# Hoisted LayerNorm statistics, a split transpose eviction and TensorE warm-up matmuls at the start of a one-core transformer block

## The chip, the cores and the metric

The kernel runs on one core of a Trainium2 chip. The metric is device time in microseconds of the whole program; lower is better. The 31 executions of the kernel before that stand beside the experiments lie within 0.36 % of each other (865.16 to 868.29 us), those of each other kernel within 0.27 %, so differences of 1 us (0.1 %) need several rounds and, better, the trace. All runs compared below are of the fast state (none is over 1.5 % above the fastest of its kernel; the largest excess is 0.37 %).

Engines are named as in the profile: PE (TensorE matmul), PEld (its weight load), ACT (ScalarE), DVE (VectorE), POOL (GpSimd), SP (SyncE, which issues the DMAs here).

## The reference

A pre-LayerNorm linear-attention block (32 heads of 32) and a gated ReLU block, bf16, 2048 tokens of width 1024, hidden width 3584:

```python
x = A_x
h  = x + _A_ref(_layernorm(x), A_wqkv, A_wo)      # pk, pq = phi(k), phi(q); kv = pk^T v; o = pq kv / (pq z)
h2 = h + _B_ref(_layernorm(h), B_W_gate, B_W_up, B_W_down)   # (relu(x Wg) * (x Wu)) Wd
# phi(t) = where(t > 0, t + 1, exp(t)) + 1e-6
```

Only the first 25 us matter: LayerNorm of the first row tiles of x (128 rows each), their transposes, and the first k projections.

## The kernel before

The program is a list of operations for each engine, and semaphores carry the dependencies between engines. On DVE the order of emission is the order of execution in the traces: in the kernel before, tile 3's x had landed at 10.5 us (issued at 3.25, 7.2 us to landing), yet its statistics, which need nothing else, ran at 18.63, behind tile 2's normalize at 17.24, before which DVE stood idle for 1.36 us.

```python
NX1 = 4                                    # buffers for x tiles

def layernorm(src_full, src_chunk_bufs, dst_ap, dst_buf, norm_eng, name):
    # DVE: bn_stats x2, bn_aggr;  POOL: ve = var + eps, rstd = ve ** -0.5, nmr = -mean * rstd
    ... (cut)
    PL.add("dve", lambda e: e.tensor_scalar(out=dst_ap, in0=src_full, scalar1=rstd[:, k, :],
                                            scalar2=nmr[:, k, :], op0=ALU.mult, op1=ALU.add), ...)

def ln1(st):
    i = st % NX1
    layernorm(x1[:, i, :], B_x1[i], xn[:, st % 2, :], B_xn[st % 2], "dve", "ln1_%d" % st)
    if st + NX1 < NST:
        load_x1(st + NX1)                  # tile 4 goes into tile 0's buffer

def T1(st):                                # 8 transposes on PE, one eviction on ACT
    (b,) = alloc_banks(P1_POOL)
    transpose8(xn[:, st % 2, :], [B_xn[st % 2]], b, NDC, "T1_%d" % st)
    evac_T("act", b, NDC, xnT[:, :, st * P:(st + 1) * P], [B_xnT[st]], "evT1_%d" % st)

def kvp_piece(st, nt):                     # 8 matmuls of 128x512, then phi: ACT exp, two DVE operations
    ... (cut)

load_x1(0, split=True); load_x1(1); load_wkv(0)     # all on the one SP queue (cut to its order)
load_x1(2); load_x1(3); load_wkv(1); load_wkv(2); load_wkv(3)

for st in range(min(2, WB)):               # WB = 4
    ln1(st)
for st in range(WB):
    T1(st)
    kvp_piece(st, 0)
    if st + 2 < WB:
        ln1(st + 2)
if WB < NST:
    ln1(WB)                                # tile 4
for nt in range(1, NKV):                   # the other pieces of tiles 0 to 3: PE has plenty to do from here
    for st in range(WB):
        kvp_piece(st, nt)
        ... (cut)
```

Of the kernel before, what the change touches and what calls it, by code (L numbers as in the profile page):

```python
# [5 lines left out]
dt = mybir.dt  # L6
ALU = mybir.AluOpType
ACTF = mybir.ActivationFunctionType
# [118 lines left out]
def bass_sequential_preLN__linear_attn_block__glu_gated_reglu__prompt_kernel(  # L127
# [10 lines left out]
    _, S, D = A_x.shape  # L138
# [3 lines left out]
    P = 128  # L142
# [3 lines left out]
    NW = min(512, D)  # L146
# [32 lines left out]
    with es:  # L179
        def sb(name, shape, dtype):  # L180
            return es.enter_context(nc.sbuf_tensor(name, list(shape), dtype))
# [43 lines left out]
        oT = RE[:, o0:o0 + NG * SBW].rearrange("p (a b) -> p a b", a=NG)  # L225
        hnT = [hnT0, hnT1]

        hsb = sb("hsb", [P, 2, STB, D], bf16)
        xn = sb("xn", [P, 2, D], bf16)
        Et = sb("Et", [P, 3, EW], bf16)  # L230
        E2t = sb("E2t", [P, 3, EW], bf16)
# [7 lines left out]
        ones_col = sb("ones_col", [P, 1], bf16)  # L239
        neghalf = sb("neghalf", [P, 1], f32)  # L240
        warm = sb("warm", [P, 8], f32)
        ip_i = sb("ip_i", [P, P], dt.int32)
        jp_i = sb("jp_i", [P, P], dt.int32)
        st6 = sb("st6", [P, NSTAT, NBC * 6], f32)
        mv = sb("mv", [P, NSTAT, 2], f32)
        ve = sb("ve", [P, NSTAT, 1], f32)
# [10 lines left out]
        def bank(b, w=512):  # L257
            return ps[:, b, 0:w]

        def bank_bf(b):  # L260
            return ps[:, b, :].bitcast(bf16).rearrange("p (a b) -> p a b", b=P)
# [17 lines left out]
        def bufs(name, n):  # L279
            return [_Buf("%s%d" % (name, i)) for i in range(n)]  # L280
# [1 line left out]
        B_bank = bufs("bank", 8)  # L282
        B_x1 = [bufs("x1_%d_" % i, NBC) for i in range(NX1)]
        B_xn = bufs("xn_", 2)
        B_xnT = bufs("xnT_", NST)
        B_wkv = bufs("wkv_", NKV)
        B_wq = bufs("wq_", ND2)
        B_wo = bufs("wo_", ND2)
# [28 lines left out]
        B_ones = _Buf("ones")  # L317
        B_neghalf = _Buf("neghalf")
        B_warm = _Buf("warm")
        B_ipi = _Buf("ipi")  # L320
        B_jpi = _Buf("jpi")

# [5 lines left out]
        def alloc_banks(pool, n=1):  # L328
            cand = sorted(pool, key=lambda b: bank_last[b])
            got = cand[:n]  # L330
            assert len(got) == n
            for b in got:
                bank_clock[0] += 1
                bank_last[b] = bank_clock[0]
            return got

        def touch_bank(b):
            bank_clock[0] += 1
            bank_last[b] = bank_clock[0]

        PL.add("pool", lambda e: e.memset(ident[:], 1.0), writes=[B_ident], name="ident1")
        PL.add(
            "pool",
# [100 lines left out]
        def mm(out_ap, lhsT, rhs, start, stop, reads, bbuf, name, skip=False):  # L444
            return PL.add(
                "pe",
                lambda e: e.matmul(out_ap, lhsT, rhs, start=start, stop=stop, skip_group_check=skip),  # L447
                reads=reads, writes=[bbuf], name=name,
            )
# [12 lines left out]
        def evac_T(eng, b, nblk, dst_ap, dst_bufs, name):  # L462
            src = bank_bf(b)[:, 0:nblk, :]
            if eng == "act":
                PL.add("act", lambda e: e.activation(out=dst_ap, in_=src, func=ACTF.Identity),  # L465
                       reads=[B_bank[b]], writes=dst_bufs, name=name)
            else:
                PL.add("dve", lambda e: e.tensor_copy(out=dst_ap, in_=src),
                       reads=[B_bank[b]], writes=dst_bufs, name=name)

        stat_ctr = [0]

        def layernorm(src_full, src_chunk_bufs, dst_ap, dst_buf, norm_eng, name):
            k = stat_ctr[0] % NSTAT
            stat_ctr[0] += 1
            for c in range(NBC):
                PL.add("dve", lambda e, c=c: e.bn_stats(out=st6[:, k, c * 6:(c + 1) * 6],  # L477
                                                        in_=src_full[:, c * BCH:(c + 1) * BCH]),
                       reads=[src_chunk_bufs[c]], writes=[B_st6[k][c]], name=name + "_bn")
            PL.add("dve", lambda e: e.bn_aggr(out=mv[:, k, :], in_=st6[:, k, :]),  # L480
                   reads=B_st6[k], writes=[B_mv[k]], name=name + "_aggr")
            PL.add("pool", lambda e: e.tensor_scalar(out=ve[:, k, :], in0=mv[:, k, 1:2], scalar1=EPS,  # L482
                                                     scalar2=None, op0=ALU.add),
                   reads=[B_mv[k]], writes=[B_ve[k]], name=name + "_ve")
            PL.add("pool", lambda e: e.tensor_tensor(out=rstd[:, k, :], in0=ve[:, k, :], in1=neghalf[:],  # L485
                                                     op=ALU.pow),
                   reads=[B_ve[k], B_neghalf], writes=[B_rstd[k]], name=name + "_rstd")
            PL.add("pool", lambda e: e.tensor_scalar(out=nmr[:, k, :], in0=mv[:, k, 0:1],  # L488
                                                     scalar1=rstd[:, k, :], scalar2=-1.0,
                                                     op0=ALU.mult, op1=ALU.mult),  # L490
                   reads=[B_mv[k], B_rstd[k]], writes=[B_nmr[k]], name=name + "_nmr")
            if norm_eng == "act":
                PL.add("act", lambda e: e.activation(out=dst_ap, in_=src_full, func=ACTF.Identity,
                                                     scale=rstd[:, k, :], bias=nmr[:, k, :]),
                       reads=list(src_chunk_bufs) + [B_rstd[k], B_nmr[k]], writes=[dst_buf], name=name + "_norm")
            else:
                PL.add("dve", lambda e: e.tensor_scalar(out=dst_ap, in0=src_full, scalar1=rstd[:, k, :],  # L497
                                                        scalar2=nmr[:, k, :], op0=ALU.mult, op1=ALU.add),
                       reads=list(src_chunk_bufs) + [B_rstd[k], B_nmr[k]], writes=[dst_buf], name=name + "_norm")

        phi_ctr = [0]

# [20 lines left out]
            col = g * P  # L523
            return ps[:, KVB[col // 512], (col % 512):(col % 512) + P]

        def ln1(st):
            i = st % NX1
            layernorm(x1[:, i, :], B_x1[i], xn[:, st % 2, :], B_xn[st % 2], "dve", "ln1_%d" % st)
            if st + NX1 < NST:
                load_x1(st + NX1)  # L530

        def T1(st):
            (b,) = alloc_banks(P1_POOL)
            transpose8(xn[:, st % 2, :], [B_xn[st % 2]], b, NDC, "T1_%d" % st)
            evac_T("act", b, NDC, xnT[:, :, st * P:(st + 1) * P], [B_xnT[st]], "evT1_%d" % st)

        def kvp_piece(st, nt):
            slot = st % NPK
            (b,) = alloc_banks(P1_POOL)
            for dc in range(NDC):  # L540
                mm(bank(b, NW), xnT[:, dc, st * P:(st + 1) * P], wkv[:, dc, nt * NW:(nt + 1) * NW],
                   dc == 0, dc == NDC - 1, [B_xnT[st], B_wkv[nt]], B_bank[b], "kvp_%d_%d" % (st, nt))
            if nt < ND2:
                phi(b, NW, pk[:, slot, nt * NW:(nt + 1) * NW], B_pk[slot][nt], "k_%d_%d" % (st, nt))
            else:
                j = nt - ND2
                PL.add("act", lambda e, b=b, j=j: e.activation(out=vv[:, slot, j * NW:(j + 1) * NW],  # L547
                                                               in_=bank(b, NW), func=ACTF.Identity),
                       reads=[B_bank[b]], writes=[B_v[slot][j]], name="v_%d_%d" % (st, j))
# [38 lines left out]
        def a1(sb_, ct, pool):  # L588
            (b,) = alloc_banks(pool)
            for dc in range(NDC):  # L590
                mm(bank(b, SBW), wq[:, dc, ct * P:(ct + 1) * P], xnT[:, dc, sb_ * SBW:(sb_ + 1) * SBW],
                   dc == 0, dc == NDC - 1, [B_wq[(ct * P) // NW]] + B_xnT[sb_ * STB:(sb_ + 1) * STB],
                   B_bank[b], "a1_%d_%d" % (sb_, ct))
            phi(b, SBW, pqT[:, sb_, ct, :], B_pqT[sb_][ct], "q_%d_%d" % (sb_, ct))

# [161 lines left out]
                if bulk:  # L757
                    bulk.pop(0)()

        for st in range(min(2, WB)):  # L760
            ln1(st)
        for st in range(WB):
            T1(st)
            kvp_piece(st, 0)
            if st + 2 < WB:
                ln1(st + 2)
        if WB < NST:
            ln1(WB)
        for nt in range(1, NKV):
            for st in range(WB):  # L770
                kvp_piece(st, nt)
                if nt == NKV - 1 and st >= 1:
                    kvacc(st - 1)
            if nt == 1:
                if WB < NST:
                    T1(WB)
                if WB + 1 < NST:
                    ln1(WB + 1)
        if NKV == 1:
            for st in range(1, WB):  # L780
                kvacc(st - 1)
            if WB < NST:
                T1(WB)
            if WB + 1 < NST:
                ln1(WB + 1)
        for st in range(WB, NST):
            if st + 1 < NST:
                T1(st + 1)
            if st + 2 < NST:
                ln1(st + 2)  # L790
            trickle(2)
            kvp(st)
            kvacc(st - 1)
# [126 lines left out]
```

## Time and profile before

| | before |
|---|---|
| device time, median of 4 (lowest to highest) | 865.92 us (865.58 to 866.59) |
| profiled span | 863.8 us |
| PE busy | 847.2 us, 98 % |
| PE busy between 25 and 855 us | 829.68 of 830 us |

The table of stretches gives, for each stretch of the span, its length, then the busy us (and instructions) of PE, PEld, DVE, ACT and POOL, the granted PE clock (the share of full clock speed that the trace records; 1.00 is full), the DMA share and GB/s. Of the kernel before:

```profile
20.00:25.00 5.00, 3.25 (x21) 1.51 (x20) 1.68 (x4) 1.62 (x2) 1.05 (x3) 1.00 0.24 73
25.00:30.00 5.00, 5.00 (x25) 2.29 (x24) 2.39 (x5) 1.79 (x3) 0.81 (x3) 1.00 0.01 3
25.00:855.00 830.00, 829.68 (x4522) 397.82 (x4521) 259.75 (x487) 166.53 (x249) 29.49 (x84) 1.00 0.39 124
```

PE is full from 25 us on, so nothing that happens later on another engine can shorten the time. What can be won lies before. The timeline of PE shows it, each line with start, length, instructions, and in brackets the idle time before them with what ended it (L457 are transposes, L447 projections). Of the kernel before:

```profile
6.70 1.01 PE L457 MATMUL ps<-ident,xn 128*128 128x128 bf16 x8 [6.70 <-DVE xn L497]
9.16 3.59 PE L447 MATMUL ps<-RB,RA 128*128 128x512 bf16 x8 [1.45 <-DMA RB<-in_A_wqkv_dram]
12.55 1.06 PE L457 MATMUL ps<-ident,xn 128*128 128x128 bf16 x8
14.72 1.90 PE L447 MATMUL ps<-RB,RA 128*128 128x512 bf16 x8 [1.12 <-ACT RA L465]
17.84 0.62 PE L457 MATMUL ps<-ident,xn 128*128 128x128 bf16 x8 [1.22 <-DVE xn L497]
19.58 1.90 PE L447 MATMUL ps<-RB,RA 128*128 128x512 bf16 x8 [1.11 <-ACT RA L465]
22.11 0.62 PE L457 MATMUL ps<-ident,xn 128*128 128x128 bf16 x8 [0.63 <-DVE xn L497]
23.85 8.81 PE L447 MATMUL ps<-RB,RA 128*128 128x512 bf16 x40 [1.12 <-ACT RA L465]
```

There are four pairs of transposes and projection, one for each tile. Eight projection matmuls take 3.59 us the first time, starting 427 ns apart, and 1.90 us later, 216 ns apart: PE starts at half clock. (The clock column reads 1.00 there all the same: the trace holds no clock record before 14.27 us. The spacing of the matmuls is the evidence: in the changed kernel it is 427 ns where the record reads 0.50, from 22.91 to 26.32 us, and 216 ns where it reads 1.00.) **The number to watch is 23.85 us**, the start of tile 3's projection: from there PE waits for 0.3 us in all until the end.

In the chain of waits (start, length, what), the last of those four steps reads as follows before the change (the pieces named "issue", under 0.1 us each, are left out here and below):

```profile
21.21 0.28 POOL nmr L488
21.51 0.56 DVE xn L497
22.11 0.64 PE ps L457 x8
22.77 1.03 ACT RA L465
23.85 8.81 PE ps L447 x40
```

Statistics, three POOL steps, normalize, transposes and eviction stand one after the other. Last, the load of tile 4, of which the kernel before takes no notice: the first line is from the timeline of SP (issue and its length), the second from the DMA view (count, size, us from issue to landing):

```profile
10.45 3.27 SPq L375 DMA_DIRECT2D RE<-in_A_x_dram  x1
RE<-in_A_x_dram SPq DMA_DIRECT2D x1, 256.0 KB, 9.7
```

It is issued at 10.45 us, behind three weight loads of 1 MB each, and lands at 20.1.

### The profile page before, as it was taken

To read this page: it belongs to the slowest core of one execution; us is meant where nothing else is said; L and a number is where in the kernel's file an instruction comes from. 1 tells how busy PE (TensorE), PEld (TensorE's weight loads), DVE (VectorE), ACT (ScalarE), POOL (GpSimd) and SP (SyncE) were. 2 spreads that over 40 slices of the span, in tenths; PEclk is the share of its full clock that TensorE was granted. 3 is DMA by queue.
4 is the path that set the end of the run, shared out by engine and by line. 5 is a ranking of instruction groups with operands and counts; after the bars stand their busy time and mean duration, and the time that the engine had idled before them with its cause. 6 is when DMAs were issued, how large, how long until landed. Compare 5 with 4: busy or idle time off the path is not lost.

```text
span 863.8 us, 10965 instructions
## 1 busy us (share of the span) xinstructions
PE 847.2 (98%) x4608; PEld 405.9 (47%) x4608; DVE 274.3 (32%) x517; ACT 173.9 (20%) x258; POOL 34.9 (4%) x107
## 2 busy tenths in 40 slices
PE   4999999999999999999999999999999999999998
PEld 2455555554544444445444444454444444444443
DVE  4534444766534321115432201343411012112111
ACT  2334443332322211001222100022221001111100
POOL 2101100000000000000000000000000000000000
PEclk9999999999999999999999999999999999999999
DMA  8156500000144336553333555334354654363052
GB/s 279 46 190 201 187 1 1 1 13 25 30 148 160 113 105 213 172 166 126 122 110 116 188 180 185 123 99 133 99 183 129 211 171 152 116 195 99 26 173 94
DMA packets 105536, 109.75 MB, mean 127 GB/s; under 512 B 2960, under 2 KB 101520, under 8 KB 105488
## 3 DMA queue, kind: packets, MB, share of 16 engines
q1 hardware_dynamic: 105488, 109.06, 39.7%
q8 instruction: 36, 0.59, 0.3%
q14 instruction: 12, 0.10, 0.0%
HBM read 104.86 MB, written 4.19 MB: 126 GB/s over the span
## 4 chain that ended last, share of the span: by engine, by line
PE 97%; DVE 1%; DMA 1%; POOL 0%; issue 0%; ACT 0%; SPq 0%; DVEq 0%
PE ps L447 95%; PE ps L457 2%; DMA RB<-in_A_wqkv_dram 1%; DVE st L477 0%; POOL rstd L485 0%; DVE RE L512 0%; SPq L375 0%; DVE xn L497 0%; ACT RA L465 0%; POOL nmr L488 0%; POOL ve L482 0%; DVE RC L705 0%; DVE hsb L648 0%; DVE mv L480 0%; ACT Et L507 0%
## 5 line engine op out<-in xcount | busy, mean ns | idle before, releaser
L447 PE MATMUL ps<-RE,gring 128*128 128x512 bf16 x896 | 198.9, 379 | 0.0
L447 PE MATMUL ps<-RC,gring 128*128 128x512 bf16 x896 | 196.3, 379 | 0.0
L447 PE MATMUL ps<-wdring,RA 128*128 128x512 bf16 x896 | 194.0, 379 | 0.0
L680 DVE TENSOR_TENSOR RA<-RC,ps 128x512 bf16<-128x512 bf16 x112 | 77.0, 687 | 262.1 <-PE ps L447 262.1
L678 ACT ACTIVATE RC<-ps 128x512 bf16<-128x512 f32 x112 | 66.9, 597 | 461.9 <-PE ps L447 461.9
L447 PEld LDWEIGHTS ps<-wdring,RA 128*128 128x128 bf16 x896 | 87.7, 98 | 105.7
L447 PEld LDWEIGHTS ps<-RC,gring 128*128 128x128 bf16 x896 | 87.0, 98 | 103.0
L447 PEld LDWEIGHTS ps<-RE,gring 128*128 128x128 bf16 x896 | 86.3, 98 | 100.1
L447 PE MATMUL ps<-RB,RA 128*128 128x512 bf16 x512 | 115.3, 383 | 4.8 <-ACT RA L465 3.3
L447 PEld LDWEIGHTS ps<-RB,RA 128*128 128x128 bf16 x512 | 49.4, 98 | 62.6 <-ACT RA L465 4.0
L705 DVE TENSOR_TENSOR RC<-ps,hsb 128x512 bf16<-128x512 f32 x32 | 20.1, 684 | 176.9 <-PE ps L447 176.9
L447 PE MATMUL ps<-RA,RC 128*128 128x512 bf16 x256 | 58.0, 379 | 0.0
L447 PE MATMUL ps<-wo,RE 128*128 128x512 bf16 x256 | 57.9, 379 | 0.0
L507 ACT ACTIVATE Et<-ps 128x512 bf16<-128x512 f32 x64 | 38.2, 597 | 88.5 <-PE ps L447 55.6
L509 DVE TENSOR_SCALAR E2t<-Et 128x512 bf16<-128x512 bf16 x64 | 18.6, 291 | 66.8 <-ACT Et L507 66.7
L447 PEld LDWEIGHTS ps<-wo,RE 128*128 128x128 bf16 x256 | 25.0, 98 | 30.2
L447 PEld LDWEIGHTS ps<-RA,RC 128*128 128x128 bf16 x256 | 24.3, 98 | 27.2
L648 DVE TENSOR_TENSOR hsb<-ps,x 128x512 bf16<-128x512 f32 x32 | 22.1, 691 | 28.8 <-PE ps L447 28.6
L482 POOL TENSOR_SCALAR ve<-mv 128x1 f32<-128x1 f32 x32 | 7.1, 221 | 580.3 <-DVE mv L480 580.3
L465 ACT ACTIVATE RE<-ps 128x1024 bf16<-128x1024 bf16 x24 | 24.5, 1022 | 24.7 <-PE ps L457 24.7
L457 PE MATMUL ps<-ident,xn 128*128 128x128 bf16 x256 | 20.4, 225 | 8.9 <-DVE xn L497 8.9
L547 ACT ACTIVATE RE<-ps 128x512 bf16<-128x512 f32 x32 | 19.1, 597 | 36.3 <-PE ps L447 36.3
(45 smaller groups left out, 323.1 us busy)
## 6 DMA issues: line engine op xcount, KB each, us to landing
gring<-in_B_W_gate_dram SPq DMA_DIRECT2D x28, 1024.0 KB, 5.4
gring<-in_B_W_up_dram SPq DMA_DIRECT2D x28, 1024.0 KB, 7.5
wdring<-in_B_W_down_dram SPq DMA_DIRECT2D x56, 512.0 KB, 3.6
RB<-in_A_wqkv_dram SPq DMA_DIRECT2D x4, 1024.0 KB, 10.9
x<-in_A_x_dram SPq DMA_DIRECT2D x16, 256.0 KB, 2.6
out_dram<-RC SPq DMA_DIRECT2D x32, 128.0 KB, 3.6
RE<-in_A_x_dram SPq DMA_DIRECT2D x15, 256.0 KB, 3.0
RC<-in_A_wqkv_dram SPq DMA_DIRECT2D x2, 1024.0 KB, 6.6
```

What stands on the lines that cost most here:

```text
L447: lambda e: e.matmul(out_ap, lhsT, rhs, start=start, stop=stop, skip_group_check=skip),
L457: lambda e, i=i: e.transpose(tb[:, i, :], src_ap[:, i * P:(i + 1) * P], ident[:]),
L465: PL.add("act", lambda e: e.activation(out=dst_ap, in_=src, func=ACTF.Identity), reads=[B_bank[b]], writes=dst_bufs, name=name)
L482: PL.add("pool", lambda e: e.tensor_scalar(out=ve[:, k, :], in0=mv[:, k, 1:2], scalar1=EPS, scalar2=None, op0=ALU.add), reads=[B_mv[k]], w ...
L507: PL.add("act", lambda e: e.activation(out=Et[:, k, 0:w], in_=src, func=ACTF.Exp), reads=[B_bank[b]], writes=[B_E[k]], name=name + "_exp")
L509: PL.add("dve", lambda e: e.tensor_scalar(out=E2t[:, k, 0:w], in0=Et[:, k, 0:w], scalar1=1.0, scalar2=1e-6, op0=ALU.min, op1=ALU.add), rea ...
L547: PL.add("act", lambda e, b=b, j=j: e.activation(out=vv[:, slot, j * NW:(j + 1) * NW], in_=bank(b, NW), func=ACTF.Identity), reads=[B_bank ...
L648: PL.add("dve", lambda e, b=b, nt=nt: e.tensor_tensor(out=hsb[:, hs, j, nt * NW:(nt + 1) * NW], in0=bank(b, NW), in1=x2[:, xs, nt * NW:(nt ...
L678: PL.add("act", lambda e: e.activation(out=rg[:, k, :], in_=bank(ga, SBW), func=ACTF.Relu), reads=[B_bank[ga]], writes=[B_rg[k]], name="rg ...
L680: PL.add("dve", lambda e: e.tensor_tensor(out=hhT[:, ft, :], in0=rg[:, k, :], in1=bank(gb, SBW), op=ALU.mult), reads=[B_rg[k], B_bank[gb]] ...
L705: PL.add("dve", lambda e, j=j, k=k: e.tensor_tensor(out=outst[:, k, :], in0=bank(banks4[j], NW), in1=hsb[:, hs, j, dh * NW:(dh + 1) * NW], ...
```

## The change

Its intent is to fill the start of the program: (1) dummy matmuls on a zero tile, so that PE is at full clock when the real work comes; (2) statistics of a tile emitted one tile ahead of its normalize, so that DVE need not wait for POOL; (3) the eviction of the transposes in two halves, so that the projection's first four matmuls may start after the first half.

```diff
+        RF = sb("RF", [P, max(2 * STB * D, 1024)], bf16)   # the h buffer; the zero tile shares it
+        zeros_t = RF[:, 0:512]
...
+        PL.add("pool", lambda e: e.memset(zeros_t[:], 0.0), writes=[B_zeros], name="zeros")
...
-        def ln1(st):
+        def ln1_stats(st):
             i = st % NX1
-            layernorm(x1[:, i, :], B_x1[i], xn[:, st % 2, :], B_xn[st % 2], "dve", "ln1_%d" % st)
+            ln1_norms[st] = layernorm(x1[:, i, :], B_x1[i], xn[:, st % 2, :], B_xn[st % 2], "dve",
+                                      "ln1_%d" % st, defer=True)
+
+        def ln1_norm(st):
+            ln1_norms.pop(st)()
             if st + NX1 < NST:
                 load_x1(st + NX1)
...
+            if split and NDC >= 2:
+                src_ = bank_bf(b)
+                PL.add("act", lambda e: e.activation(out=xnT[:, 0:HDC, st * P:(st + 1) * P], in_=src_[:, 0:HDC, :],
+                                                     func=ACTF.Identity), ...)     # first half
+                PL.add("act", ...)                                                 # second half
...
+        def pe_dummies(n):
+            (b,) = alloc_banks(P1_POOL)
+            for _ in range(n):
+                mm(bank(b, 512), zeros_t[:, 0:P], zeros_t[:, 0:512], True, True, [B_zeros], B_bank[b], "dummy")
...
-        for st in range(min(2, WB)):
-            ln1(st)
+        NDUM0, NDUM1 = 14, 5
+        pe_dummies(NDUM0)
+        ln1_stats(0)
+        if WB > 1:
+            ln1_stats(1)
+        ln1_norm(0)
         for st in range(WB):
-            T1(st)
+            T1(st, split=True)
+            if st == 0:
+                pe_dummies(NDUM1)
+            if st + 2 < NST:
+                ln1_stats(st + 2)
+            if st + 1 < NST:
+                ln1_norm(st + 1)
             kvp_piece(st, 0)
-            if st + 2 < WB:
-                ln1(st + 2)
-        if WB < NST:
-            ln1(WB)
... (later tiles: statistics one tile earlier in the same way)
```

## The prediction

> **What bounds the kernel now.** TensorE. The page has PE busy 847.2 of 863.8 us; the stretch table gives 829.68 busy of 830 us between 25 and 855 us. Only the first 25 us have idle PE time that this change touches: 11.65 us busy there. The timeline shows why: T1 of tile 0 at 6.70 waits for its normalize, the first projection at 9.16 for wkv_0's landing, then each of tiles 1 to 3 pays phi, statistics, three POOL steps, normalize, transposes and eviction in series. The last PE gap ends at 23.85, when tile 3's first projection starts. After that PE is never short of work, so the change is worth what it moves 23.85, and no more.
>
> **What it removes and adds, costed from the trace.**
> - Clock: the first eight projection matmuls take 3.61 us, later eights 1.90; the transposes 1.01 to 1.06, later 0.62. [...] Fourteen dummies (about 4.5 to 6 us, estimated) should remove the slow eights: about 2.1 us in all.
> - Hoisted statistics: normalize no longer waits 1.36 us for POOL in tiles 2 and 3.
> - Split eviction: 1.02 us becomes about 0.6 before the first four matmuls may start, 0.4 a tile.
> Together some 5 us, if the inputs were there. They aren't.
>
> **What it moves into the way.** VectorE runs in order, and the hoisted statistics now stand before an earlier tile's normalize, waiting for a DMA. From issue times plus times to landing in the DMA view: tile 1 lands at 6.1, tile 2 at 9.8, tile 3 at 10.5, and tile 4, issued at 10.45 behind three 1 MB weight loads on the same queue, at 20.1.
> - stats(1) before norm(0): norm 0 ends near 8.25 instead of 6.55. T1 of tile 0 then follows, then five dummies, so the first projection starts near 10.0 instead of 9.16, but runs in 1.75 us instead of 3.6.
> - stats(2) before norm(1): norm 1 ends near 11.9 instead of 9.9; T1 of tile 1 starts at 12.0 (before 12.55).
> - Tile 2's projection starts near 16.8 (before 19.58): the gain shows here, almost 3 us.
> - stats(4) before norm(3): it cannot start before 20.1. Then 1.28 + 0.21 + 0.05 us statistics, 0.55 normalize: norm 3 ends at 22.2, T1 of tile 3 starts at 22.3 (before 22.11) and tile 3's projection at 23.6 (before 23.85).
> So the whole gain is given back waiting for tile 4's load; 0.25 us remain, from the split eviction less the late normalize.
>
> **Prediction.** 865.8 us, range 864.8 to 867.6. Faster by over 2%: 0.005; within 2%: 0.99; slower: 0.005.
>
> **What would show it.** In the timeline: BN statistics starting at about 6.1, 9.8 and 20.1, each released by a DMA; PE idle from about 18.5 to 22.3; the first projection's eight matmuls in about 1.8 us; the 25 to 855 stretch as full as before; the load of tile 4 in the chain of waits in place of POOL steps.
>
> **What would make it wrong.** [...] if the clock falls back, tile 3's transposes and projections run at half speed and the time is 1 to 2.5 us worse (about one chance in four; no trace yet shows a fallback). If tile 4 lands earlier, by changed order on the queue, up to 3 us could be gained. The aliasing of the zero tile with the h buffer and the moved banks should cost nothing, as both are idle then.

## The result, and the profile after

| | before | after |
|---|---|---|
| device time, median (lowest to highest) | 866.17 us, 13 runs (865.34 to 868.34) | 866.93 us, 9 runs (866.02 to 867.67) |
| profiled span | 863.8 us | 865.2 us |
| PE busy | 847.2 us | 852.4 us |
| tile 3's projection starts | 23.85 us | 24.13 us |
| granted clock of the whole span | 1.000 | 0.998 |

The ratio after/before is 1.0006, with a 95 % interval from 0.9997 to 1.0015. (Ratios are the mean time of one kernel's fast runs over that of the other's fast runs of the same rounds, so not quite the ratio of the medians.) Nothing was gained; the interval also holds a small loss. The 5.2 us more of busy PE are, on balance, dummies. One warning on these rows: the profiled execution of before held full clock (1.000), and most of its other executions did not (0.998 in 20 of 31, see e4). That is the likely reason why the spans differ by 1.4 us and the medians by only 0.8.

The stretches of the changed kernel, same columns:

```profile
20.00:25.00 5.00, 1.68 (x11) 0.87 (x12) 4.26 (x10) 1.08 (x2) 1.39 (x3) 0.79 0.19 60
25.00:30.00 5.00, 5.00 (x22) 2.17 (x21) 1.76 (x5) 1.19 (x2) 1.23 (x3) 0.87 0.23 56
25.00:855.00 830.00, 829.68 (x4519) 397.81 (x4518) 255.68 (x481) 166.53 (x249) 30.43 (x81) 1.00 0.39 124
```

From 25 us on PE is as full as before, but the granted clock in the first two stretches is 0.79 and 0.87. "Busy" does not tell fast from slow. (The profile's own 40 slices are 21.6 us long, and their clock row prints 9 throughout: the fall is too short to be seen there.) The timeline of PE of the changed kernel, without the lines between that bear on nothing here (dummies and projections are L451, transposes L461):

```profile
1.36 5.39 PE L451 MATMUL ps<-RF 128*128 128x512 bf16 x14 [1.36 <-POOL RF L344]
7.44 0.61 PE L461 MATMUL ps<-ident,xn 128*128 128x128 bf16 x8 [0.68 <-POOL ve L486]
9.66 1.90 PE L451 MATMUL ps<-RB,RA 128*128 128x512 bf16 x8 [0.53 <-DMA RB<-in_A_wqkv_dram]
13.61 1.90 PE L451 MATMUL ps<-RB,RA 128*128 128x512 bf16 x8 [0.69 <-ACT RA L562]
16.69 1.90 PE L451 MATMUL ps<-RB,RA 128*128 128x512 bf16 x8 [0.73 <-ACT RA L562]
22.63 0.81 PE L461 MATMUL ps<-ident,xn 128*128 128x128 bf16 x8 [4.05 <-DVE xn L504]
24.13 9.87 PE L451 MATMUL ps<-RB,RA 128*128 128x512 bf16 x40 [0.69 <-ACT RA L562]
```

The parts do what they were meant to do: the first projection takes 1.90 us instead of 3.59, the eviction wait is 0.69 to 0.73 instead of 1.12, and tile 2's projection starts at 16.69 instead of 19.58. The change is 2.9 us ahead there. Then PE is idle for 4.05 us, and behind the gap the transposes take 0.81 instead of 0.62 us and the 40 projection matmuls 9.87 instead of 8.81. Five lines of the timeline, four of DVE and one of POOL (15.92), show what PE waited for:

```profile
5.35 1.29 DVE L481 BATCH_NORM_STATS2 st<-RE 128x6 f32<-128x512 bf16 x2 [0.65 <-DMA RE<-in_A_x_dram]
10.30 1.29 DVE L481 BATCH_NORM_STATS2 st<-RE 128x6 f32<-128x512 bf16 x2 [3.01 <-DMA RE<-in_A_x_dram]
15.92 0.26 POOL L492 TENSOR_SCALAR nmr<-mv,rstd 128x1 f32<-128x1 f32 x1
20.64 1.28 DVE L481 BATCH_NORM_STATS2 st<-RE 128x6 f32<-128x512 bf16 x2 [3.44 <-DMA RE<-in_A_x_dram]
22.08 0.49 DVE L504 TENSOR_SCALAR xn<-RE,rstd,nmr 128x1024 bf16<-128x1024 bf16 x1
```

Tile 3's scale and shift were ready at 16.18 us (15.92 + 0.26), but its normalize runs at 22.08: in DVE's list it stands behind the statistics of tile 4, and these wait for tile 4's load. In the chain of waits the load has taken the place of the POOL steps (a 0.04 us piece of DVE at 21.95 is left out too):

```profile
10.88 9.73 DMA RE<-in_A_x_dram
20.64 1.30 DVE st L481 x2
22.08 0.51 DVE xn L504
22.63 0.83 PE ps L461 x8
24.13 9.87 PE ps L451 x40
```

The sum closes: tile 3's projection starts 0.28 us later (24.13 against 23.85) and the 40 matmuls take 1.06 us longer; together 1.34 us, and the profiled spans differ by 1.4 us.

### The profile page after: what moved, and what is told of

It reads as the page before. It is cut to its first block, busy times and chain, and to the rows that moved or that the text cites. A ratio compares the mean times of both kernels' runs of the same rounds, so it can differ in the third digit from the quotient of the medians.

```text
span 865.2 us, 11008 instructions
## 1 busy us (share of the span) xinstructions
PE 852.4 (99%) x4627; PEld 407.5 (47%) x4627; DVE 272.7 (32%) x517; ACT 174.0 (20%) x262; POOL 38.3 (4%) x108
## 4 chain that ended last, share of the span: by engine, by line
PE 96%; DMA 1%; SPq 1%; DVE 1%; issue 0%; POOL 0%; ACT 0%; DVEq 0%
PE ps L451 94%; PE ps L461 2%; DMA RE<-in_A_x_dram 1%; SPq L379 1%; DVE st L481 0%; DVE xn L504 0%; DVE RC L750 0%; DVE RF L693 0%; ACT RA L562 0%; POOL rstd L489 0%; POOL nmr L492 0%; DVE mv L484 0%; POOL ve L486 0%; DVEq L112 0%; SPq L112 0%
## 5 line engine op out<-in xcount | busy, mean ns | idle before, releaser
L451 PE MATMUL ps<-RE,gring 128*128 128x512 bf16 x896 | 198.9, 379 | 0.0
L451 PE MATMUL ps<-RC,gring 128*128 128x512 bf16 x896 | 196.3, 379 | 0.0
L451 PE MATMUL ps<-wdring,RA 128*128 128x512 bf16 x896 | 194.0, 379 | 0.0
L451 PEld LDWEIGHTS ps<-wdring,RA 128*128 128x128 bf16 x896 | 87.6, 98 | 105.8
L451 PEld LDWEIGHTS ps<-RC,gring 128*128 128x128 bf16 x896 | 87.0, 98 | 102.9
L451 PEld LDWEIGHTS ps<-RE,gring 128*128 128x128 bf16 x896 | 86.3, 98 | 100.1
L451 PE MATMUL ps<-RB,RA 128*128 128x512 bf16 x512 | 114.7, 382 | 2.6 <-ACT RA L562 2.1
L451 PEld LDWEIGHTS ps<-RB,RA 128*128 128x128 bf16 x512 | 49.3, 98 | 60.5 <-ACT RA L562 2.7
L750 DVE TENSOR_TENSOR RC<-ps,RF 128x512 bf16<-128x512 f32 x32 | 20.2, 684 | 176.9 <-PE ps L451 176.9
L451 PE MATMUL ps<-RA,RC 128*128 128x512 bf16 x256 | 58.0, 379 | 0.0
L451 PE MATMUL ps<-wo,RE 128*128 128x512 bf16 x256 | 57.9, 379 | 0.0
L451 PEld LDWEIGHTS ps<-wo,RE 128*128 128x128 bf16 x256 | 25.0, 98 | 30.2
L451 PEld LDWEIGHTS ps<-RA,RC 128*128 128x128 bf16 x256 | 24.3, 98 | 27.1
L486 POOL TENSOR_SCALAR ve<-mv 128x1 f32<-128x1 f32 x32 | 10.0, 311 | 578.3 <-DVE mv L484 578.3
L693 DVE TENSOR_TENSOR RF<-ps,x 128x512 bf16<-128x512 f32 x32 | 22.1, 691 | 28.8 <-PE ps L451 28.6
L461 PE MATMUL ps<-ident,xn 128*128 128x128 bf16 x256 | 19.7, 220 | 5.8 <-DVE xn L504 5.1
```

What stands on the lines that cost most here:

```text
L451: lambda e: e.matmul(out_ap, lhsT, rhs, start=start, stop=stop, skip_group_check=skip),
L461: lambda e, i=i: e.transpose(tb[:, i, :], src_ap[:, i * P:(i + 1) * P], ident[:]),
L486: PL.add("pool", lambda e: e.tensor_scalar(out=ve[:, k, :], in0=mv[:, k, 1:2], scalar1=EPS, scalar2=None, op0=ALU.add), reads=[B_mv[k]], w ...
L693: PL.add("dve", lambda e, b=b, nt=nt: e.tensor_tensor(out=hsb[:, hs, j, nt * NW:(nt + 1) * NW], in0=bank(b, NW), in1=x2[:, xs, nt * NW:(nt ...
L750: PL.add("dve", lambda e, j=j, k=k: e.tensor_tensor(out=outst[:, k, :], in0=bank(banks4[j], NW), in1=hsb[:, hs, j, dh * NW:(dh + 1) * NW], ...
```

## The experiments

Two theories. **Theory A**: the gain is given back because tile 4's hoisted statistics wait for a load and hold up tile 3's normalize. **Theory C**: on top of that, the idle gap makes PE's clock fall back, which costs over 1 us. Rivals: the load only happens to land when other work is done (B); the dummies delay the first projection (D); the split evictions harm or help by themselves (E, F).

The results together; ratios are to the kernel before in the same rounds.

| kernel | median us | ratio (95 % interval) |
|---|---|---|
| the change (first measurement) | 866.93 | 1.0006 (0.9997 to 1.0015) |
| the change again (e9) | 867.05 | 1.0008 (0.9996 to 1.0020) |
| change, tile 4's statistics late (e1) | 860.74 | 0.9938 (0.9925 to 0.9950) |
| change, fifth x buffer (e2) | 860.90 | 0.9941 (0.9929 to 0.9954) |
| change, gap filled with dummies (e3) | 864.83 | 0.9985 (0.9971 to 1.0000) |
| change without dummies (e4) | 865.67 | 0.9992 (0.9978 to 1.0007) |
| before + dummies (e5) | 863.99 | 0.9977 (0.9963 to 0.9991) |
| before + split eviction (e6) | 864.82 | 0.9985 (0.9972 to 0.9999) |
| e1 without dummies (e7) | 863.01 | 0.9964 (0.9950 to 0.9978) |
| pipelined by arrival (e8) | 858.31 | 0.9911 (0.9896 to 0.9926) |
| hoisting alone (e10) | 865.67 | 0.9997 (0.9985 to 1.0009) |
| e8 without dummies (e11) | 860.75 | 0.9941 (0.9929 to 0.9953) |

All gave correct results, and all are within 2 % of before. Each experiment was run in 5 rounds.

### e1: the same change, tile 4's statistics behind tile 3's normalize

```diff
         for st in range(WB):
             T1(st, split=True)
             ...
-            if st + 2 < NST:
+            late = st + 2 >= NX1
+            if st + 2 < NST and not late:
                 ln1_stats(st + 2)
-            if st + 1 < NST:
+            if late:
+                for s_ in ([3] if st == 2 else [4, 5]):
+                    if s_ == 3:
+                        ln1_norm(3)
+                    else:
+                        ln1_stats(s_)
+                if st == 3:
+                    ln1_norm(4)
+            elif st + 1 < NST:
                 ln1_norm(st + 1)
             kvp_piece(st, 0)
```

> The changed kernel with one order altered on VectorE: statistics of tile 4 come after the normalize of tile 3 (which had been ready since about 16 us), everything else kept. Theory A (the gain is given back waiting for tile 4's load at 20.6 us): transposes of tile 3 start at about 18.6 us instead of 22.63, tile 3's first projection at about 19.9 instead of 24.13, no clock fallback (granted clock 1.00 at 20 to 30 us), time 4.0 us under before, that is about 862.2. Rival B (the early stage is limited by PE, phi and eviction work, and the load only happens to land then): the projection moves by under 1 us and the time stays within 1 us of the changed kernel.

Measured: 860.74 us, ratio 0.9938: 5.1 us under before by the medians (865.88 there), where 4.0 were expected. The timeline of PE of e1, tile 3's transposes and projection:

```profile
17.95 0.61 PE L461 MATMUL ps<-ident,xn 128*128 128x128 bf16 x8
19.29 8.81 PE L451 MATMUL ps<-RB,RA 128*128 128x512 bf16 x39 [0.73 <-ACT RA L562]
```

No idle time stands before the transposes, and the clock is 1.00 throughout. Moving three DVE instructions was worth 6 us against the change. Rival B falls.

### e2: the same order, but the load moved

A fifth buffer lets tile 4 be loaded ahead of the later weight loads. It lies in the h buffer, which is idle at that time.

```diff
-        NX1 = 4
+        NX1 = 5
+        NX1R = 4                       # four in the old place
...
+        def x1(i):
+            return x1r[:, i, :] if i < NX1R else RF[:, 1024:1024 + D]
```

> The changed kernel with its order kept and the load moved: a fifth x buffer (in the h buffer's idle space) lets tile 4 be loaded ahead of the three later weight loads, so that it lands near 11.2 us instead of 20.6. Theory A: statistics of tile 4 start at about 17.2 us without a wait, transposes of tile 3 at about 19.4, its projection at about 20.6, no fallback, 3.2 us under before, about 863. A is only right if this and the altered order both gain; if the altered order gains and this does not, it is the place of the statistics' own 1.5 us on VectorE that counts and not the load. Rival B: within 1 us of the changed kernel.

Measured: 860.90 us, ratio 0.9941. Tile 4's statistics, in the order that had cost everything, no longer wait, as the timelines of SP (first line: the load is issued at 3.73 us instead of 10.88) and of DVE show (no idle time in brackets):

```profile
3.73 0.46 SPq L384 DMA_DIRECT2D RF<-in_A_x_dram  x1
15.71 1.28 DVE L486 BATCH_NORM_STATS2 st<-RF 128x6 f32<-128x512 bf16 x2
17.15 0.49 DVE L509 TENSOR_SCALAR xn<-RE,rstd,nmr 128x1024 bf16<-128x1024 bf16 x1
```

e1 changed the order and left the load, e2 the reverse; both gain the same. So it is the pair, DVE's order and a late load, and not the statistics' own 1.5 us. The expected 3.2 us were too few because I placed these statistics at 17.2 us; they ran at 15.71, as the tiles ahead of them were faster than I had reckoned.

### e3: the wait stays, the gap is filled

```diff
         for st in range(WB):
+            if st == 3:
+                pe_dummies(14)
             T1(st, split=True)
```

> The changed kernel with 14 more dummy matmuls between tile 2's projection and tile 3's transposes, that is in the 4.05 us gap of PE; the wait for tile 4's load stays. Theory C (1.3 us of the changed kernel's loss is the clock's fallback at half rate after the gap): granted clock 1.00 at 20 to 30 us, transposes of tile 3 in 0.62 us, the 40 matmuls after it in 8.8 us instead of 9.87, time 1.2 us under the changed kernel, 865.5 to 866. Rival: if the fallback costs nothing on the path, the time stays that of the changed kernel.

Measured: 864.83 us, ratio 0.9985. The timeline of PE of e3:

```profile
16.86 3.19 PE L451 MATMUL ps<-RF 128*128 128x512 bf16 x14
21.12 0.62 PE L461 MATMUL ps<-ident,xn 128*128 128x128 bf16 x8 [1.07 <-DVE xn L504]
22.43 8.81 PE L451 MATMUL ps<-RB,RA 128*128 128x512 bf16 x39 [0.69 <-ACT RA L562]
```

PE still waits for DVE, but at full clock: 0.62 and 8.81 us instead of 0.81 and 9.87. By the trace the fallback cost 1.25 us. The times of this run and of the change's differ by about 2 us; in the profiled execution of e3 tile 4's statistics started at 19.12 us, against 20.64 in the change's and 21.16 in e9's, so part of that may be an earlier load. The timelines of SP of e3, the change and e9 show where the difference comes from:

```profile
9.36 3.27 SPq L379 DMA_DIRECT2D RE<-in_A_x_dram  x1
10.88 3.27 SPq L379 DMA_DIRECT2D RE<-in_A_x_dram  x1
11.42 3.28 SPq L379 DMA_DIRECT2D RE<-in_A_x_dram  x1
```

From issue to landing the load takes 9.7 us in all three. It is the issue that moves: SP issues tile 4's load when it is done with the last weight load, whose own issue began at 5.79, 7.47 and 8.19 us (in the change the issue of that 1 MB load took SP 3.28 us, to 10.75, and tile 4's began at 10.88). Why SP is up to 2 us later with these in some executions is not settled.

### e4: the change without its dummies

```diff
-        NDUM0, NDUM1 = 14, 5
+        NDUM0, NDUM1 = 0, 0
```

> The changed kernel without its 14 + 5 dummies. Theory A with C: the first eight projection matmuls are slow again (3.6 us), so PE reaches the wait for tile 4's load later (at about 20.2 instead of 18.6 us), the gap shrinks to about 2.4 us[...]; transposes of tile 3 start at 22.5 in 0.62 us, projection at 23.8, time equal to before within 0.5 us, so about 1 us faster than with dummies, granted clock of the whole run 1.000. Rival D (dummies shorten the start as intended): without them the time is about 2 us worse than the changed kernel.

Measured: 865.67 us, ratio 0.9992. The direction was right: taking the warm-up away makes the change about 1.2 us faster (1.0006 against 0.9992 to before; the intervals overlap). Rival D's 2 us loss is not there; in the change's own timeline the first projection waits last for the weight load (0.53 us) and not for the dummies. But the expectation that the clock would hold (1.000) was wrong in three of the five executions, the profiled one among them. The gap was 1.92 us, and the clock still fell. The table of stretches of e4, cut at the times at which the clock changed:

```profile
15.70:19.11 3.41, 2.37 (x16) 1.15 (x16) 1.28 (x3) 1.56 (x3) 1.21 (x3) 1.00 1.09 364
19.11:22.53 3.42, 0.77 (x9) 0.49 (x10) 3.27 (x7) 1.29 (x3) 1.40 (x3) 1.00 0.25 71
22.53:25.94 3.41, 3.05 (x8) 1.21 (x10) 1.34 (x4) 0.40 (x1) 1.24 (x3) 0.50 0.43 126
```

The half-clock stretch is 3.41 us long. In the 3.41 us before it PE was busy for 0.77 us, 23 %: it was not idle for the whole window. The same reading of the start of every trace that has clock records, in windows of 3.41 us counted from its clock changes (which lie whole multiples of that apart, here 10.24 and 3.41 us):

| kernel | busy share of the window that ended with a fall | longest PE wait that reaches into it |
|---|---|---|
| the change | 8 % | 4.05 us |
| the change again (e9) | 18 % | 4.00 us |
| split only (e6) | 21 % | 2.01 us |
| change without dummies (e4) | 23 % | 1.92 us |
| dummies only (e5) | 29 % | 1.59 us |

Every window there at full clock that did not end with a fall was at least 49 % busy (the lowest is in the kernel before). Falls also stand at the end of traces, when PE has finished (at 864.19 us in the kernel before, at 866.00 in the change), and two of these (e7's and e8's) came after windows that were 37 % busy. The stretches that lie nearest to each other, the first of before, where the clock held, the other two of e7, where it fell:

```profile
21.10:24.51 3.41, 1.66 (x14) 0.76 (x13) 1.53 (x3) 1.62 (x2) 0.27 (x2) 1.00 0.27 77
857.71:861.12 3.41, 1.25 (x6) 0.39 (x4) 1.69 (x3) 0.00 (x0) 0.00 (x0) 1.00 0.45 154
861.12:861.95 0.83, 0.00 (x0) 0.00 (x0) 0.00 (x0) 0.00 (x0) 0.00 (x0) 0.50 0.00 0
```

So in these runs the clock fell after windows of up to 37 % and held after windows of 49 % and more; no window that was read lies between. Transposes are counted as busy here; without them (0.62 us in the window of before) the one that held would have 30 %, less than the 37 % that fell. Going up, windows of 77 % and less did not bring full clock in these traces; windows at 80 % went both ways (the change's, 22.91 to 26.32 us, did; e7's did not); those of 81 % and more did (the lowest is in the kernel before, 2.75 us of 10.86 to 14.27).

Single executions show the same fall from another side. A clock of 0.998 over the whole run amounts to one such window at half clock (0.002 x 865 / 0.5 = 3.5 us, an estimate; the traces show 3.41). Of the 31 executions of the kernel before that stand beside these experiments, 11 have 1.000 and took 865.16 to 865.28 us; 20 have 0.998 and took 865.60 to 868.29. So the clock fell before the change too, and the profile of before is of the luckier kind. In e4, three executions fell (865.67 to 866.36 us) and two did not (864.25 and 864.48). The change and e9 fell in all 16 of theirs, in 11 of them by what amounts to two windows (0.996); e1, e2 and e3 have 1.000 in all 15.

### e5 and e6: dummies alone, split alone

```diff
+        pe_dummies(14)                 # e5: the changed file with the old schedule put back, and these dummies
         for st in range(min(2, WB)):
             ln1(st)
         for st in range(WB):
             T1(st)
+            if st == 0:
+                pe_dummies(5)
```

```diff
-            T1(st)
+            T1(st, split=True)         # e6: the old schedule put back, with this alone
```

> The kernel before with the 14 + 5 dummies alone: old order on VectorE, whole evictions. Theory A with C: the statistics of tile 4 still stand behind everything that tile 3 needs, so no load is waited for and the warm clock's gain survives: first projection in 1.9 instead of 3.6 us, which is on the serial chain through phi, statistics and normalize, so tile 3's projection starts 1.8 us earlier (about 22.0 us) and the time is 1.8 us under before. Rival: dummies cost as much as they save (they delay the first projection), time within 0.5 us of before.

> The kernel before with the split eviction alone. In the trace of before, VectorE (phi, statistics, normalize) sets the pace of tiles 1 to 3 and only the last eviction, tile 3's, is on the chain: 0.4 us under before. Rival E (each of three evictions is on the chain): 1.2 us under before. Rival F (two smaller ScalarE instructions delay the exponentials): at or above before.

Measured: e5 863.99 us, ratio 0.9977: about 1.6 to 2.0 us under before, where 1.8 were expected. In the old order the dummies pay, although the clock fell in three of its six executions (864.57 to 864.70 us, against 863.33 to 863.41 in the other three), in the profiled one at 17.62 us. e6: 864.82 us, ratio 0.9985 with an interval that reaches from 0.1 to 2.4 us under before. That rules out rival F and does not tell 0.4 from 1.2 us; the split's own value stays open.

### e7: the late order without dummies

```diff
# e1, and:
-        NDUM0, NDUM1 = 14, 5
+        NDUM0, NDUM1 = 0, 0
```

> The altered order of the first experiment (statistics of tile 4 after the normalize of tile 3), without dummies. Theory A: with no load to wait for, the first projection's slow clock is on the path again: 1.7 us worse than the same order with dummies (about 862.4 us), where in the changed kernel the dummies brought nothing or a loss. Rival: dummies are worthless in this order too, time within 0.4 us of it.

Measured: 863.01 us, ratio 0.9964; e1 had 0.9938. Here the same 19 dummies are worth about 2.3 us (0.0026 of 866), where in the change they brought nothing or a loss. In the profiled execution of e7 the windows of projections were 77 and 80 % busy and stayed at half clock, so the first two projections took 3.57 and 3.59 us; the expected 1.7 us counted only one of them. e7's executions fall into two groups, 861.87 to 862.44 and 863.57 to 863.74 us, three each; the profile is of the slower one. That the faster three had only one slow projection is likely but not traced.

### e8 and e11: a version that beats both

```diff
-        for st in range(WB):
-            T1(st, split=True)
-            ... (the change's loop)
+        ln1_stats(0)
+        ln1_norm(0)
+        ln1_stats(1)
+        T1(0, split=True)
+        pe_dummies(NDUM1)
+        ln1_norm(1)
+        T1(1, split=True)
+        ln1_stats(2)
+        ln1_stats(3)
+        ln1_norm(2)
+        kvp_piece(0, 0)
+        ln1_norm(3)
+        kvp_piece(1, 0)
+        T1(2, split=True)
+        kvp_piece(0, 1)                # filler while tile 2 is evicted
+        T1(3, split=True)
+        kvp_piece(2, 0)
+        ln1_stats(4)                   # behind everything that tiles 0 to 3 need
+        kvp_piece(3, 0)
+        ln1_norm(4)
+        ln1_stats(5)
         for nt in range(1, NKV):
-            for st in range(WB):
+            for st in range(1 if nt == 1 else 0, WB):
```

e11 is e8 with both dummy counts at 0.

> A version meant to beat both: dummies and split kept; statistics emitted only where the tile has landed; transposes of tile 1 before the first projection, of tiles 2 and 3 one projection ahead of their use, with tile 0's second projection piece filling PE while tile 2 is evicted. If the theory of the early stage holds (after the load wait, what is left is 0.7 us of eviction wait and about 0.1 to 0.6 us of others per tile on PE), PE is full from about 9.9 us on and the time is about 3 us under the altered order, 857.8 us. Rival: wkv_1 or tile 2 lands too late for this and the gain is under 1 us.

> The pipelined version without its dummies: is the warm clock worth its 19 dummies there? With no load to wait for, the first windows of projections run at half rate until one window was over 80% busy: 1.8 to 3.0 us worse than 858.3, about 860.6. If the dummies cost as much as they bring: within 0.4 us of 858.3.

Measured: e8 858.31 us (4 runs from 858.20 to 858.32), ratio 0.9911, 7.3 us under the median of before in its rounds; e11 860.75 us. From the second transposes on PE is not idle again at the start, as a stretch of e8 shows:

```profile
9.93:25.00 15.07, 15.07 (x88) 7.60 (x89) 11.87 (x26) 7.22 (x13) 3.26 (x10) 1.00 0.79 255
```

In e11 the first 16 projection matmuls took 5.28 us, in e8 3.62. Here the dummies are worth 2.4 us by the medians (860.75 less 858.31) and 2.6 by the ratios; the two ran in different rounds. e8's 4 runs also lie within 0.12 us, where those of the change spread over 1.65. That tile 4's load and the clock falls are off e8's path fits this, but is not the whole account: e1 fell in no execution either, and its five still spread over 1.05.

### e9 and e10: the change once more, and hoisting alone

e9 is the changed kernel itself. e10 has no dummies and whole evictions:

```diff
-        NDUM0, NDUM1 = 14, 5
+        NDUM0, NDUM1 = 0, 0
...
-            T1(st, split=True)
+            T1(st)
```

> The changed kernel itself once more, as the measure for the others on one chip. Theory A with C: PE idle in the window before tile 3's transposes (under 30% busy), so the clock falls for at least one window of 3.4 us in the profiled run, granted clock of the run 0.998 or less; tile 4's statistics wait for its load; time between before - 0.5 and before + 1.3 us, depending on when the load lands and how the windows fall.

> Of the change, the hoisted statistics alone: no dummies, whole evictions. Theory A: tile 3 still waits for tile 4's load, then needs 1.0 instead of 0.6 us of eviction, so its projection starts about 0.4 us later than in the version without dummies; time at before or up to 1 us over it. Rival (hoisting is what gains, dummies and split do the harm): 1.4 us or more under before.

Measured: e9 867.05 us, ratio 1.0008; clock 0.998; tile 4's statistics released by the DMA at 21.16 us. It repeats the result on another set of rounds. e10 865.67 us, ratio 0.9997: hoisting alone gains nothing. In its profiled execution PE ran at half clock until 18.58 us (3.57 and 3.60 us for the first two projections, 1.90 for the third) and was itself the brake, so tile 4's statistics began at 20.21 without any wait. The rival, 1.4 us under before, falls; that the load was the limit in this run too is not shown by its trace.

## Why the prediction was right or wrong

The measured 866.93 us lie inside the range, 1.1 us above the predicted 865.8. They lie inside because the range left room for a fallback of the clock; that it came in every execution was not foreseen. Point by point:

- **PE bounds the kernel, and only the start counts: right.** 829.68 of 830 us busy before and after.
- **The gain is real until tile 2: right.** Tile 2's projection was expected near 16.8 us and started at 16.69.
- **The whole gain is given back waiting for tile 4's load: right, and shown** by e1 and e2, which take away one half of the cause each and gain 5 us. Tile 3's transposes were expected at 22.3 and started at 22.63; its projection at 23.6, started at 24.13. The 0.25 us that were to remain became a loss of 0.28, because the load landed about 0.5 us later in that execution (20.6 against 20.1 us; it was issued at 10.88 instead of 10.45) and the transposes ran partly at half clock (0.81 against 0.62 us).
- **Single times on the way were off by up to 1 us.** The first normalize was expected to end near 8.25 and ended at 7.29 (tile 1 landed at 5.35 and not 6.1); neither is on the path, since the wait behind tile 4 absorbs it.
- **The clock's fallback was mis-sized in its chance.** The prediction gave it one in four, an estimate: no trace then showed a fall. The reported clock lies between 0.996 and 0.998 in all ten recorded executions of the changed kernel and in e9's six. It is 1.000 in the profiled one of before, from whose trace the prediction was made, but 0.998 in 20 of 31 others. The estimate was too low. The runs show falls after windows that were up to 37 % busy, and at the start with waits as short as 1.59 us. Its size, 1 to 2.5 us, was right: 1.25 us in the profiled execution, where one window of 3.41 us ran at half rate; in e4 and e5 the executions that fell took 1.2 to 2.1 us longer than those that did not. A clock of 0.996 over 865 us amounts to two such windows (0.004 x 865 / 0.5 = 6.9 us); where the second lies was not traced.

Two orders on which the argument rests stand in the trace of the change. DVE kept the order of its list: tile 3's normalize had its operands ready at 16.18 us and ran at 22.08, behind tile 4's statistics. And tile 4's load landed behind the weight load issued before it: that one, issued at 7.47 us, landed at 20.0, and tile 4's, a quarter of its size and issued at 10.88, at 20.6. e2 cured it by issuing earlier, at 3.73.

## What to carry to other kernels

Before an operation is hoisted on DVE, write beside it when its input lands: here a hoisted operation that waited until 20.64 us held up the normalize behind it, which had been ready since 16.18, and a three-instruction reordering was worth 6 us. Warm-up matmuls pay only if the time that they save is not waited away again: the same 19 dummies brought 1.6 to 2.6 us in the three orders where tile 4's load was not waited for (e5, e1 against e7, e8 against e11), and nothing or a loss where it still set the pace. Read the granted clock and the length of a fixed group of matmuls in short stretches, since busy shares and long slices show a half-speed PE as busy: in the change 5.00 of 5.00 us at a clock of 0.87, and 9 in every 21.6 us slice of the clock row.
